# Attention whose row sums travel by DMA and whose results are divided where they lie, with new written orders for a quad of heads

## The chip, the cores and the metric

The kernel runs on one core of a Trainium2 chip. A core has five engines that run side by side, each through its own queue of instructions in program order: TensorE (PE in the profile; its weight loads are PEld), VectorE (DVE), ScalarE (ACT), GpSimd (POOL) and SyncE (SP), which here issues nearly all DMAs. Engines wait for each other by semaphores. TensorE's results go to PSUM, of which this stage uses eight banks of 128 x 512 fp32; all else lies in SBUF or in DRAM. The metric is the device time of one execution in microseconds (us), a median over runs.

## The reference

```python
mod = (_silu(c) @ w_mod).reshape(c.shape[0], 6, 1, -1)
sa, ca, ga, sb, cb, gb = (mod[:, 0], mod[:, 1], mod[:, 2], mod[:, 3], mod[:, 4], mod[:, 5])
h = _layernorm(x) * (1 + ca) + sa
x = x + ga * _A_ref(h, A_wq, A_wk, A_wv, A_wo)      # attention
h = _layernorm(x) * (1 + cb) + sb
x = x + gb * _B_ref(h, B_w1, B_b1, B_w2, B_b2)      # layernorm, 4608 wide gelu MLP

# _A_ref: 32 query heads of 18 columns, one shared key and value head
scores = einsum("bhqd,bkd->bhqk", q, k) * (Dh ** -0.5)
p = _softmax(scores, axis=-1)
o = einsum("bhqk,bkd->bhqd", p, v)
return o.transpose(0, 2, 1, 3).reshape(B, S, H * Dh) @ wo
```

All tensors are fp32. S = 2048 rows, D = 576 columns, H = 32 heads, Dh = 18.

## The kernel before, in words

The program has three stages: the first norm with the projections (to about 130 us), attention (to about 1360 us) and the MLP. The change is in attention.

**A quad.** The 2048 query rows are four blocks of 512 (tb), the 32 heads are eight quads of four heads (qd); quad n = 8 tb + qd, 32 in all. The tile qst of a quad holds its queries, split into high and low parts so that 64 rows of TensorE carry one head: rows 0 to 63 one pair of heads (g = 0), rows 64 to 127 the other (g = 1). Two of the 64 rows hold the negated maximum of each query's scores, so that the product gives the scores less the maximum.

**An order written out by hand.** The loop at the end of the listing runs for each quad through a string of tokens: QUAD for quads 0 to 8, QUADW for 9 to 30, LAST for 31. Each token is work that is issued at that place, in the same order on every engine's queue:

- S0, S1 (st_mm): one score matmul of 64 x 128 keys by 512 queries into a bank of psB (four banks), then ScalarE's exp from there into P (line 966). 64 of them a quad.
- M0, M1 (mx_mm): one score matmul of a coming quad into psM (three banks), then VectorE's maximum over it (line 986). X1 and R1 are a pair that handles two key blocks in one: ScalarE's relu of the product with a key difference (line 977), then VectorE's addition and maximum (line 984). 48 M and 8 of each of X1 and R1 a quad. The digit is g.
- V2, V3, V4 (pv_mm, line 954): two, three or four of the 64 units of P times V of a quad, each unit 128 columns of a chunk for four heads. They run eight units behind the scores. V has 32 columns of which 18 are values; the others are ones, so that row 18 of each head's 32 rows of the result is the row sum of the exponentials.
- F1, F2 (smax_fin1, smax_fin2): the maxima of the next quad. F1 reduces them on VectorE, F2 turns them on TensorE (line 358), ScalarE and VectorE write two parts, and four DMAs (line 365) put them into the next quad's qst.
- WO: one half row tile of the output projection (14 matmuls, line 753) of a finished block, and its addition to x.
- T1, RC, T2, OS: each takes post_quad (lines 763 to 803), which works off a finished quad, one step further.

After every fourth V unit, `between` issues what has no token: the load of the quad after next (load_q, six DMAs), one step of the generators in `fill` (first late_weights, then ln2_rows) and one or two steps of weight_parts, which splits the MLP's weights on GpSimd and stores them to DRAM. In the chunks named by `quiet` (the two before F2 and the one before RC) weight_parts rests.

**post_quad before.** When the last V unit of a quad is issued, ScalarE copies the result from PSUM to O (128 x 512: for each of four heads 32 rows, by 512 queries). T1: VectorE turns O in blocks of 32 x 32 (line 771), so that the row sums become column 18 of each block of T. RC: VectorE takes the reciprocal of those, GpSimd multiplies T by them (line 775). T2: VectorE turns T back into O (line 777). OS: ScalarE rounds O to fp32r (line 789), GpSimd takes the rest (line 790), and four DMAs put both into the attention tile A (lines 794 to 801).

**ln2_tile before.** When both halves of a row tile of x have their output projection, ln2_rows is added to `fill` for tiles of the first two blocks (eight tiles). ln2_tile (lines 582 to 630) takes the second norm, scales it, takes the MLP's own norm, all step by step, and then TensorE turns the 128 x 576 tile by five transposes (transpose_tile, line 156); ScalarE copies four of them from PSUM to yr, VectorE the fifth. The steps marked "T" are held back until a WO token. The tiles of the other two blocks are normed in the MLP stage by ln2_stages, where VectorE turns the tile in blocks of 32 x 32, four DMAs put it to DRAM (`turned`) so that the blocks land turned, and three DMAs fetch it into yr.

## Time and profile before

| | |
|---|---|
| median of 3 runs | 2215.54 us (2215.16 to 2216.22) |
| the profiled execution | 2216.44 us, of it span 2214.7 us |
| granted TensorE clock | 0.999 |
| instructions | 46128 |
| DMA, mean over the span | 141 GB/s |

The profile's span runs from the first to the last instruction. Busy time is the union of an engine's instructions. The page's groups name a line, the engine, the operation, what is written and read with shapes, the count, then busy time and the mean of one. A row of a timeline is a start, a duration and a group; rows of one line that follow each other are merged. An engine's idle time is put down to what ended it.

### The profile page before, as it was taken

What the parts mean: (1) busy time and instruction counts of PE and PEld (TensorE: products, weight loads), DVE (VectorE), ACT (ScalarE), POOL (GpSimd) and SP (SyncE); (2) the same over time, 40 slices, a digit from 0 to 9 for tenths busy, and PEclk for the clock granted to TensorE, in tenths of its full rate; (3) what the DMA queues carried; (4) which work ended last, traced back from release to release, by engine and by line L of the source; (5) the groups of instructions that cost most, each with busy time, mean ns of one, the idle gap of its engine ahead of it and who ended that gap; (6) DMA issues with size and microseconds to landing.
All of it is one profiled execution on the core that took longest, in us unless ns stands there. A gap on an engine that the chain in (4) does not pass through costs nothing.

```text
span 2214.7 us, 46128 instructions
## 1 busy us (share of the span) xinstructions
PE 2195.2 (99%) x16599; PEld 1446.6 (65%) x16599; DVE 1936.6 (87%) x3421; ACT 1629.8 (74%) x3122; POOL 1524.4 (69%) x1768
## 2 busy tenths in 40 slices
PE   8999999999999999999999999999999999999999
PEld 6654444444544545445454445898988899889898
DVE  7589999999999999999999992888888878787887
ACT  5579999999999999999999998544445444343443
POOL 7654456666776687677676640888899767877676
PEclk9999999999999999999999999999999999999999
DMA  6233143443333332333333321666767746676663
GB/s 228 87 133 92 34 134 117 135 130 113 126 121 120 116 130 95 114 130 112 116 117 121 127 71 59 200 195 190 201 187 201 207 131 180 184 219 189 177 184 122
DMA packets 209082, 312.71 MB, mean 141 GB/s; under 512 B 39023, under 2 KB 99839, under 8 KB 208853
## 3 DMA queue, kind: packets, MB, share of 16 engines
q1 hardware_dynamic: 208709, 309.60, 45.0%
q8 instruction: 132, 2.16, 0.4%
q14 instruction: 97, 0.79, 0.1%
q10 hardware_dynamic: 144, 0.15, 0.0%
HBM read 203.30 MB, written 96.15 MB: 135 GB/s over the span
## 4 chain that ended last, share of the span: by engine, by line
PE 96%; DVE 1%; ACT 1%; issue 1%; POOL 1%; DMA 0%; SPq 0%; ACTq 0%; DVEq 0%; POOLq 0%
PE psC L954 24%; PE psB L1178 18%; PE psA L1281 16%; PE psB L964 14%; PE psM L320 13%; PE psB L753 2%; PE psB L249 2%; PE psB L974 2%; PE psA L1315 1%; PE psA L320 1%; PE psA L753 1%; PE psB L156 0%; DVE mx L345 0%; PE psB L358 0%; PE psM L964 0%
## 5 line engine op out<-in xcount | busy, mean ns | idle before, releaser
L966 ACT ACTIVATE P<-psB 128x512 f32<-128x512 f32 x2013 | 1055.0, 620 | 42.5 <-PE psM L320 19.7
L986 DVE TENSOR_REDUCE mx<-psM 128x1 f32<-128x512 f32 x1476 | 934.3, 682 | 28.6 <-PE psM L320 13.6
L964 PE MATMUL psB<-qst,KS 64*128 64x512 f32 x2013 | 605.1, 433 | 0.1
L320 PE MATMUL psM<-KS,qst 64*128 64x512 f32 x1722 | 590.0, 434 | 0.7 <-DVE mx L338 0.2
L954 PE MATMUL psC<-P,V 128*32 128x256 f32 (+3 forms) x6608 | 568.2, 439 | 0.0
L964 PEld LDWEIGHTS psB<-qst,KS 64*128 64x128 f32 x2013 | 301.9, 184 | 218.7 <-ACT P L966 185.3
L320 PEld LDWEIGHTS psM<-KS,qst 64*128 64x128 f32 x1722 | 283.6, 184 | 185.6 <-DVE mx L986 130.9
L1178 PE MATMUL psB<-ops,w1a 128*128 128x512 f32 x1512 | 393.8, 396 | 0.2 <-DVE h L1193 0.2
L1178 PEld LDWEIGHTS psB<-ops,w1a 128*128 128x128 f32 x1512 | 270.1, 188 | 46.8 <-DVE h L1193 0.6
L954 PEld LDWEIGHTS psC<-P,V 128*32 128x32 f32 x6608 | 147.0, 108 | 187.4 <-issue 159.9
L1287 DVE TENSOR_TENSOR XT<-psA,XT 128x576 f32<-128x576 f32 x330 | 241.4, 752 | 16.2 <-PE psA L1281 10.8
L1281 PEld LDWEIGHTS psA<-w2s,big 128*128 128x128 f32 x1584 | 223.7, 188 | 12.1 <-DVE XT L1287 0.2
L1281 PE MATMUL psA<-w2s,big 128*128 128x288 f32 x1584 | 230.1, 294 | 0.0
L1255 POOL TENSOR_TENSOR big<-s,big 128x512 fp32r<-128x512 f32 x132 | 171.0, 1296 | 10.6
L984 DVE CUSTOM_DVE_ANT_0 xc<-psM,xc 128x512 f32<-128x512 f32 x246 | 166.2, 682 | 12.6 <-PE psB L964 4.6
L1191 ACT ACTIVATE psB<-gs 128x512 f32<-128x512 f32 x144 | 86.7, 602 | 120.7 <-DVE gs L1190 120.7
L1187 ACT ACTIVATE h<-psB,b1t 128x512 f32<-128x512 f32 x144 | 97.9, 680 | 105.1 <-PE psB L1178 98.6
L790 POOL TENSOR_TENSOR os<-O,os 128x512 fp32r<-128x512 f32 x31 | 39.8, 1284 | 171.4 <-ACT os L789 171.4
L977 ACT ACTIVATE xc<-psB 128x512 f32<-128x512 f32 x246 | 154.5, 628 | 2.8 <-PE psM L320 0.2
L1190 DVE SCALAR_TENSOR_TENSOR gs<-psB,h 128x512 f32<-128x512 f32 x144 | 98.9, 687 | 38.6 <-ACT psB L1188 38.5
L824 POOL TENSOR_TENSOR r<-r,r 128x256 fp32r<-128x256 f32 (+1 forms) x162 | 121.8, 752 | 13.0
L1196 ACT ACTIVATE big<-h 128x512 fp32r<-128x512 f32 x39 | 24.7, 634 | 139.5 <-DVE h L1193 139.5
(216 smaller groups left out, 3306.0 us busy)
## 6 DMA issues: line engine op xcount, KB each, us to landing
w1a<-w1scr SPq DMA_DIRECT2D x252, 256.0 KB
w2s<-w2sum SPq DMA_DIRECT2D x132, 288.0 KB
w1scr<-r SPq DMA_DIRECT2D x126, 256.0 KB
w2s<-w2scr SPq DMA_DIRECT2D x76, 288.0 KB
w2scr<-r SPq DMA_DIRECT2D x72, 288.0 KB
w2sum<-r SPq DMA_DIRECT2D x72, 288.0 KB
...
```

The costliest lines, as they stand in the source:

```text
L320: pe.matmul(o, QST[n][64 * g:64 * g + 64, p, 128 * qt:128 * (qt + 1)], KS[64 * g:64 * g + 64, 512 * kb:512 * (kb + 1)], start=True, stop=True)
L824: po.tensor_tensor(o[:, n:2 * n], src, o[:, :n].bitcast(F32), op=ALU.subtract)
L954: pe.matmul(PVt[n][32 * j:32 * (j + 1), cs], V[:, kc, :], t[:, j, cs], start=(kc == 0 and h0 == 0), stop=(kc == 15), skip_group_check=True)
L964: pe.matmul(t, KS[64 * g:64 * g + 64, 128 * kc:128 * (kc + 1)], QST[n][64 * g:64 * g + 64, i, :], start=True, stop=True)
L966: ac.activation(P[n, kc][:, 2 * i + g, :], t, AF.Exp, scale=SCALE)
L977: ac.activation(XC[-1], t, AF.Relu)
L984: ve.tensor_tensor_reduce(c, t, c, 1.0, -3.0e38, ALU.add, ALU.max, o)
L986: ve.tensor_reduce(o, t, axis=AX.X, op=ALU.max)
L1178: pe.matmul(o, x, y, start=(first and i == 0), stop=(i == len(terms) - 1), skip_group_check=True)
L1255: po.tensor_tensor(unit(u, 1), x, unit(u, 0).bitcast(F32), op=ALU.subtract)
L1281: pe.matmul(p[:, i, :288], x[:, ts_], W2S[k][:, y], start=(bool(first) and q == 0), stop=(q == 2), skip_group_check=True)
L1287: ve.tensor_tensor(o, p[:, :, :288], o, op=ALU.add)
```

## The change

- post_quad no longer turns O for quads 0 to 29. A new generator, divide, takes its place. At T1 a DMA gathers the four rows of sums (512 each) from O into R, 128 partitions of 16. At RC VectorE takes the reciprocals in place, and a DMA stores them to DRAM (rscr). At T2 a DMA reads them back, each head's row spread over its 32 partitions (T, 128 x 512). At OS GpSimd multiplies O by T where it lies.
- In these quads GpSimd also rounds O to fp32r, where ScalarE did, and a new token OD, right behind F2, issues the DMAs into A. Quads 30 and 31 go the old way.
- QUAD and QUADW are new orders of the same numbers of S, M, X, R, and of 64 V units, with OD added. LAST is unchanged.
- ln2_tile turns its tile by VectorE in place and by DMAs through DRAM, as ln2_stages does, into a new scratch turnedA. The steps "T" are gone, and so are the PE transposes and the copies from PSUM. The branch for tiles with tb of 2 or more, which this function never sees, is gone too, and with it the norm of the 64 columns that were kept twice.

```diff
+        ve.transpose(h, h)
+        yield
+        for p in range(0, 128, 32):
+            sy.dma_start(turned0.rearrange("(c f) n -> f c n", f=32)[:, :, p:p + 32],
+                         h[p:p + 32].rearrange("f (c n) -> f c n", n=32))
+        yield
+        yield
+        yr = YR[tb // 2][:, KD * (tb % 2):KD * (tb % 2 + 1), 128 * t:128 * (t + 1)]
+        sy.dma_start(yr[:, :KD - 1], turned0[:512].rearrange("(k p) n -> p k n", p=128))
+        for q in range(2):
+            sy.dma_start(yr[64 * q:64 * q + 64, KD - 1], turned0[512:])
         yield
...
+    def divide(n, O):
+
+        R = px.tile([128, 16], F32, name="R", bufs=2)
+        sy.dma_start(R, O[DH::32].rearrange("j (i c) -> j i c", c=16))
+        yield
+        ve.reciprocal(R, R)
+        sy.dma_start(rscr[n % 2].rearrange("j (i c) -> (j i) c", c=16), R)
+        yield
+        T = px.tile([128, 16, 32], F32, name="T").rearrange("p a b -> p (a b)")
+        sy.dma_start(T, rscr[n % 2][:, None, :].to_broadcast([4, 32, TB]))
+        yield
+        po.tensor_mul(O, O, T)
...
-        ac.activation(os[:, 0], O, AF.Copy)
+        if n < NQT - 2:
+            e.tensor_copy(os[:, 0], O)
+        else:
+            ac.activation(os[:, 0], O, AF.Copy)
         e.tensor_tensor(os[:, 1], O, os[:, 0].bitcast(F32), op=ALU.subtract)
+        if n < NQT - 2:
+            yield
...
-    QUAD = """S0 M0 S1 S1 M0 V3 S0 M1 S1 M0 M1 S0 V3 M0 S1 M1 S0 V2 M0 S1 S1 M0 X1 S0 V4 T1 X1 M0 M1 M0 S1 S0
-            V4 S1 RC M0 S1 S0 M0 S0 M1 V3 S0 M1 R1 S1 S0 M0 X1 V3 M0 S1 S1 R1 S0 M0 S1 V3 M0 X1 M0 S0 S1 S0
-            M1 V3 M0 S1 S1 M0 S0 R1 S0 V3 R1 S0 S1 M1 S0 M0 X1 V3 M0 S1 M0 S1 S0 S0 R1 V3 M0 X1 S0 M1 S0 M1
-            V3 S1 M0 M0 S1 T2 S0 S1 V4 M0 S1 S0 M1 S0 M1 V3 S0 R1 S1 M0 F1 S1 S0 V3 X1 M0 S1 M0 R1 S0 F2 OS
-            V4 M0 M1 S0 S1 M0 X1 V4 S1 M0 S1 S0 M1 M0 S1 V2 R1 S0 M1 S0 V2 S0 S1 M0 M1 V2 S1""".split()
-    QUADW = """M1 M1 S0 S0 X1 S1 M0 V4 S1 M0 S1 S0 M1 M0 V4 M0 S1 S0 M0 S1 T1 M0 X1 V4 S1 RC S0 S0 M1 M0 S1 V4
-            S0 R1 M1 S0 S1 M0 S1 V3 S1 M0 S0 X1 M0 M0 S1 V2 M0 S1 S0 R1 V2 M0 X1 M0 S1 S0 S1 M0 V4 S0 T2 R1
-            M0 S1 OS S0 M1 WO S0 R1 M1 S0 M1 S0 X1 V3 S0 M1 M0 S1 S1 M1 S0 V3 M0 S1 S0 R1 S0 M0 X1 V3 M0 S1
-            X1 M0 S1 M0 S1 V4 S1 M0 R1 S0 M1 S0 V4 S0 M1 M0 F1 S1 S0 S1 V4 M0 S1 M0 X1 S0 M1 F2 V4 M1 S0 S0
-            S1 M0 S1 M0 V3 R1 S0 S0 S1 R1 M0 V3 S0 S1 M0 S1 M0 S1 V3 M0 S1 M1 S0 M1 S0 V3""".split()
+    QUAD = """S1 S0 M1 S0 V4 M0 S1 M0 S1 S0 M1 V4 S1 M0 M1 S0 S1 S0 M1 V4 X1 M0 R1 S0 X1 M0 S0 T1 V3 S1 M0 S1 S0
+            M1 M0 S1 V3 M1 S0 S1 M0 X1 M0 S1 V3 M0 S1 M0 S1 S0 M1 V3 M0 S1 S0 S0 R1 M1 S0 V3 S1 M0 S0 S1 R1 S1
+            M0 V3 M0 X1 S0 S1 M1 M0 S1 V3 M1 S0 RC S0 X1 R1 M0 S1 V3 S1 M0 S0 R1 S0 M0 S1 V4 S0 M1 S0 X1 M0 X1
+            M0 T2 V4 M0 S1 M0 R1 S0 S1 S0 V4 X1 M0 S0 R1 S1 M0 OS V3 M0 S1 S0 S1 M1 S0 V4 F1 M0 S1 M0 M1 S0 S1
+            F2 OD V3 S0 R1 S0 S1 M1 S1 M0 V3 M0 S1 S1 S0 M0 M1 S0 V3 S0 M1 M0""".split()
+    QUADW = """S1 M0 S1 S0 S1 M0 V4 S1 M0 X1 M0 M1 S0 V4 S0 S1 M0 S1 S0 M1 M0 V4 S1 M0 M1 S0 S0 M0 S1 T1 V3 X1 M0
+            S1 M1 S0 R1 S0 V4 X1 M0 S1 M1 M0 S1 S0 V4 S0 M1 S0 R1 S1 M1 S0 V3 S0 R1 X1 M0 S1 S0 M1 V3 M0 S1 M0
+            X1 S1 R1 S0 V4 S0 RC S1 M0 S1 M0 M1 V3 S0 S1 S1 M0 M0 X1 V4 S0 R1 S0 R1 M0 S1 WO S0 M1 M0 M0 S1 S1
+            S0 T2 V3 M0 S1 S0 S0 M1 M0 X1 V4 S0 M1 S1 M0 S1 M0 S1 OS V3 M0 S0 M1 S0 S1 M0 F1 S1 V4 R1 S0 S1 M0
+            X1 M0 F2 OD V3 S1 M0 M1 S0 S0 S1 M0 V3 M1 S0 S0 S1 R1 M1 S0 V4 M0""".split()
```

What each order has of V tokens, groups and places:

| | QUAD before | QUAD after | QUADW before | QUADW after |
|---|---|---|---|---|
| V4, V3, V2 | 5, 12, 4 | 7, 12, 0 | 9, 8, 2 | 10, 8, 0 |
| V units done at T1, RC, T2 | 12, 16, 40 | 12, 33, 40 | 8, 12, 27 | 12, 33, 40 |
| V units done at OS, F2, OD | 50, 50, - | 48, 55, 55 | 27, 48, - | 47, 54, 54 |
| V units done at WO | - | - | 27 | 40 |

More of the change, by code (lines that the diff above doesn't have):

```diff
@@ L501, in block_kernel @@
     WO, YR, ATT, B2 = {}, {}, {}, {}
+    rscr = [dr.tile([4, TB], F32, name="rscr%d" % i) for i in range(2)]
     woscr = dr.tile([2, 128, D], F32, name="woscr")
@@ L650, in ln2_rows @@
         if tb % 2 and t == NT - 1:
+            yield
+            yield
             R = YR[tb // 2]
@@ L769, in post_quad @@
         yield
-        T = px.tile([128, 16, 32], F32, name="T")
-        ve.transpose(T.rearrange("p a b -> p (a b)"), O)
-        yield
-        R = px.tile([128, 16], F32, name="R", bufs=2)
-        ve.reciprocal(R, T[:, :, DH])
-        e.tensor_tensor(T, T, R[:, :, None].to_broadcast([128, 16, 32]), op=ALU.mult)
-        yield
-        ve.transpose(O, T.rearrange("p a b -> p (a b)"))
-        yield
+        if n < NQT - 2:
+            yield from divide(n, O)
+        else:
+            T = px.tile([128, 16, 32], F32, name="T")
+            ve.transpose(T.rearrange("p a b -> p (a b)"), O)
+            yield
+            R = px.tile([128, 16], F32, name="R", bufs=2)
+            ve.reciprocal(R, T[:, :, DH])
+            e.tensor_tensor(T, T, R[:, :, None].to_broadcast([128, 16, 32]), op=ALU.mult)
+            yield
+            ve.transpose(O, T.rearrange("p a b -> p (a b)"))
+            yield
         if tb not in ATT:
```

37 lines of the change are left out of this document (12 added, 25 removed).

## The prediction

> **What bounds the kernel now.** I read the page first, for the engine that ends last:
>
> ```profile
> PE 2195.2 (99%) x16599; PEld 1446.6 (65%) x16599; DVE 1936.6 (87%) x3421; ACT 1629.8 (74%) x3122; POOL 1524.4 (69%) x1768
> ...
> PE 96%; DVE 1%; ACT 1%; issue 1%; POOL 1%; DMA 0%; SPq 0%; ACTq 0%; DVEq 0%; POOLq 0%
> PE psC L954 24%; PE psB L1178 18%; PE psA L1281 16%; PE psB L964 14%; PE psM L320 13%; PE psB L753 2%; PE psB L249 2%; PE psB L974 2%; PE psA L1315 1%; PE psA L320 1%; PE psA L753 1%; PE psB L156 0%; DVE mx L345 0%; PE psB L358 0%; PE psM L964 0%
> ```
>
> The chain of waits is nearly all TensorE. Its attention lines (954, 964, 320, 974, 753) make some 55% of the span. A busy PE isn't a PE at its peak, so I cut the attention stage into single quads of heads, each from its first V group to the next quad's, and asked for the busy time of every engine in five of them. The columns are the stretch, its length, then PE, PEld, DVE, ACT and POOL busy, the clock, the DMA share and GB/s:
>
> ```profile
> 317.90:355.29 37.39, 37.39 (x365) 18.50 (x361) 36.54 (x71) 36.97 (x76) 25.28 (x37) 1.00 0.40 133
> 355.29:392.69 37.40, 37.40 (x365) 18.47 (x361) 36.55 (x71) 36.96 (x76) 22.44 (x36) 1.00 0.36 120
> 943.01:982.27 39.26, 39.26 (x346) 19.21 (x343) 37.86 (x75) 37.30 (x76) 31.86 (x46) 1.00 0.40 134
> 982.27:1022.19 39.92, 39.92 (x351) 19.82 (x348) 38.03 (x76) 37.86 (x77) 24.33 (x33) 1.00 0.32 105
> 1180.39:1219.65 39.26, 39.26 (x346) 19.27 (x344) 37.08 (x72) 37.28 (x76) 23.81 (x35) 1.00 0.33 111
> ```
>
> The first two follow QUAD, the others QUADW. The last and the third take the same 39.26 us although VectorE works 0.8 us less and GpSimd 8 us less in one: neither sets the length. ScalarE is within 0.4 us of it in QUAD. The fourth holds the five PE transposes of a norm tile and is 0.66 us longer.
>
> Is PE itself full? I priced its groups by where the next one starts, in the timeline of PE, and show those stretches by themselves: V4, a seven-op group (four on one half of the rows), V3, a six-op group (three and three), V2, a four-op group, and the 14 matmuls of a WO:
>
> ```profile
> 814.87:815.87 1.00, 1.00 (x11) 1.00 0.00 0
> 815.87:816.99 1.12, 1.12 (x11) 1.00 0.05 15
> 816.99:817.78 0.79, 0.79 (x11) 1.00 0.03 5
> 821.24:822.14 0.90, 0.90 (x11) 1.00 0.99 379
> 351.60:352.16 0.56, 0.56 (x9) 1.00 0.04 7
> 352.16:352.83 0.67, 0.67 (x8) 1.00 0.03 6
> 522.76:524.82 2.06, 2.06 (x16) 1.00 0.00 0
> ```
>
> S, M, X and R with digit 0 use rows 0 to 63, with digit 1 rows 64 to 127, and the halves run side by side: two, three and four in the longer half give 0.67, 0.90 and 1.12, so a group costs 0.21 + 0.23 for each in its longer half. The rest of a quad is waiting, and these rows of weight loads (stretch 470 to 1300, 21 quads) say for whom:
>
> ```profile
> L964 PEld LDWEIGHTS psB<-qst,KS 64*128 64x128 f32 x1344 | 201.4, 184 | 157.2 <-ACT P L966 139.7 <-issue 3.5 <-ACT xc L977 3.0
> L320 PEld LDWEIGHTS psM<-KS,qst 64*128 64x128 f32 x1176 | 194.9, 184 | 130.4 <-DVE mx L986 89.8 <-DVE mx L984 13.1 <-issue 12.8
> ```
>
> Loads wait for ScalarE to free psB and VectorE to free psM; most of that lies under the matmul in flight.
>
> **The orders, counted.** QUADW before has 9 V4, 8 V3 and 2 V2: 9.00 + 6.32 + 1.12 = 16.44. Its groups between them, the one with WO counted as two, are 20, with 69 in the longer halves: 4.20 + 15.87. With WO 2.06 and the transpose of the maxima 0.21 (timeline below) that is 38.78; measured 39.26, so 0.48 of waiting. After: 10 V4 and 8 V3 (16.32), 19 groups with 71 (the closing M0 joined to the next quad's first group): 3.99 + 16.33, and 2.27 again: 38.91. QUAD before: 5 V4, 12 V3, 4 V2 (16.72), 21 groups with 68 (4.41 + 15.64), 0.21: 36.98, measured 37.39, so 0.41 waiting. After: 7 V4 and 12 V3 (16.48), 19 groups with 71 (20.32), 0.21: 37.01. So the new orders give PE no less work: 0.13 more in each of 22 quads, 0.03 in 9, 2.86 + 0.27, together **+3.13 us**. They can gain only from the waiting, 22 x 0.48 + 9 x 0.41 = 14.25 us in all.
>
> **The norm tiles.** Of eight tiles these go:
>
> ```profile
> L156 PE MATMUL psB<-ident,Z x40: 270/272/274, 603.6 to 1158.3; 128*128 128x128 f32 x40
> ...
> L166 ACT ACTIVATE yr<-psB x8: 597/602/603, 604.3 to 1158.5; 128x512 f32<-128x512 f32 x8
> L168 DVE COPY yr<-psB x8: 291/292/294, 604.4 to 1158.6; 128x128 f32<-128x128 f32 x8
> ```
>
> PE gets back 39.92 - 39.26 = 0.66 each: 8 x 0.66 = **-5.28 us**, the surest term, as it comes off the bounding engine. In their place come one VectorE transpose of 128x576 and seven DMAs a tile. From 0.70 for 512 columns (below) the transpose is an estimated 0.79, so VectorE pays 0.50 net in a quad in which it drops 1.4; the cover is psM's three banks, and without it PE would lose up to those 0.50 in eight quads, 4 us. For the DMAs the stage after attention has the same step:
>
> ```profile
> L696 SPq DMA_DIRECT2D turned<-BC x32: 382/536/1148, 1473.9 to 1749.3; - x32
> ```
>
> Four puts are 2.1 us of SP's time, at the end of a quad, behind the maxima's DMAs; the rows of quads above have the DMA engines at 0.32 to 0.40. Nobody in attention reads yr, so I cost them at nothing. If they held the queue, the next quad's load would be late by those 2.1 us, and it has a quad to spare.
>
> **The division.** What goes, and its neighbours:
>
> ```profile
> L771 DVE STREAM_TRANSPOSE T<-O x21: 700/703/705, 473.1 to 1263.8; 128x512 f32<-128x512 f32 x21
> L774 DVE RECIPROCAL R<-T x21: 231/234/238, 474.3 to 1265.0; 128x16 f32<-128x16 f32 x21
> L775 POOL TENSOR_TENSOR T<-T,R x21: 1042/1048/1060, 477.5 to 1265.8; 128x512 f32<-128x512 f32 x21
> L777 DVE STREAM_TRANSPOSE O<-T x21: 654/700/704, 482.8 to 1273.5; 128x512 f32<-128x512 f32 x21
> ```
>
> ```profile
> L794 SPq DMA_DIRECT2D big<-os x76: 764/800/886, 486.2 to 1279.5; - x76
> L789 ACT ACTIVATE os<-O x21: 632/661/672, 484.1 to 1274.8; 128x512 fp32r<-128x512 f32 x21
> L790 POOL TENSOR_TENSOR os<-O,os x21: 1276/1285/1305, 484.8 to 1275.6; 128x512 fp32r<-128x512 f32 x21
> ```
>
> VectorE drops 0.70 twice, ScalarE 0.66. GpSimd multiplies two full tiles (as L790, 1.29) instead of T by R (1.05), and copies os:
>
> ```profile
> L823 POOL CAST r<-w2b 128x288 fp32r<-128x288 f32 x85 | 36.0, 424 | 20.7 <-DMA w2scr<-r 8.7 <-DMA w2sum<-r 6.7 <-DMA w1scr<-r 2.8
> ```
>
> That is 0.42 x 512/288 = 0.75, so +1.0 us a quad on 31.9 of 39.3: hidden, until GpSimd passes PE. Three DMAs are new. The trace has no gather of 64-byte pieces and no such broadcast; the nearest are the four small qst<-ms below (0.70 to issue, about 1.4 to land) and, for the 256 KB broadcast, a load of 72 KB on the chain:
>
> ```profile
> 40.90 3.53 DMA qst<-qscr
> ```
>
> So 2.1 to 3.5 us each, perhaps 5 for the broadcast; I take 3.5, the larger transfer. The tokens leave 21 of 64 V units (12.9 us) for the gather and 7 (4.3 us) for the store, and 4.3 for the broadcast. The reciprocal waits for the gather with the maxima behind it, but with 9 us to spare; the multiply waits with only GpSimd's weight parts behind it, which has 7 us idle a quad. Cost: nothing, and none below, since PE touches no part of it.
>
> What it buys is waiting. ScalarE's 0.66 and VectorE's 1.4 are each more than the 0.41 or 0.48 to be had, but in QUAD ScalarE is still at 36.3 of 37.0, so not all goes. I take three quarters: 14.25 x 0.75 = **-10.69 us**, an estimate between none and all.
>
> **The maxima's way to the next quad** is what the new orders tighten. The rows of PE, of SP, and of a tenth of a microsecond in which the last of four DMAs moves:
>
> ```profile
> 814.66 0.28 PE L358 MATMUL psB<-ident,mxf 128*16 128x128 f32 x1
> 814.87 1.06 PE L954 MATMUL psC<-P,V 128*32 128x512 f32 x8
> ...
> 823.21 0.47 PE L964 MATMUL psB<-qst,KS 64*128 64x512 f32 x1
> ```
>
> ```profile
> 816.06 2.79 SPq L365 DMA_DIRECT2D qst<-ms  x4
> ```
>
> ```profile
> 819.50:819.60 0.10, 0.10 (x6) 0.05 (x2) 0.10 (x3) 0.10 (x1) 0.00 (x0) 1.00 0.21 36
> ```
>
> From the transpose (F2) to landing: 819.60 - 814.66 = 4.94 us; the next quad's first score comes 3.6 us later still. After the change QUADW has behind F2 only 0.21, V3, seven, V3, seven, V4: 0.21 + 0.79 + 1.12 + 0.79 + 1.12 + 1.00 = 5.03, and QUAD 4.82 and one 0.23 step. So 0.1 us is left of 3.6. I cost it at nothing; what it costs beyond that is a rival.
>
> The last of the four is issued at 816.06 + 2.79 - 0.70 = 818.15, so its data move 1.45 us after the issue, and by these rows the margin holds. The Trainium skill, "DMA: Bandwidth & Descriptors", section "Anatomy of one DMA — SWDGE (gpsimd) path", gives one DMA some 2.0 us of fixed time, most of it the wait for the receipt of the write, and so speaks against this edit. By that figure, an estimate from that page, the last row would be there at 820.15, 5.49 behind F2 and 0.46 past the margin, and the sum would be 2199.1 (rival 1) + 31 x 0.46 = 2213.4; the burst speaks for less, but shows data and no receipt.
>
> **Sum.** The profiled execution took 2216.44 us (span 2214.7), 0.9 above the median of the runs: 2216.44 + 3.13 - 5.28 - 10.69 = 2203.60, or 2202.7 as a median.
>
> **Rivals.**
> 1. All the waiting goes: 2215.5 + 3.1 - 5.3 - 14.25 = 2199.1. My prices are read to 0.01 us, and half of that in 37 groups of 31 quads is 5.7: 2193. For it: both engines are relieved by more than the wait. Against: ScalarE's 98% in QUAD.
> 2. The waiting stays, being a matter of three or four banks: 2215.5 + 3.1 - 5.3 = 2213.3. For it: VectorE's 0.8 less between two quads above moved nothing.
> 3. The burst shows the data move, not PE being told. If that came a quarter of the way from the burst's 1.45 to the 3.53 that the chain shows for a landing, 0.52 us later, it would be 0.43 past the margin. PE standing there lets the others catch up, so it adds to 2199.1: 31 x 0.43 = 13.3, 2212.4. For it: the chain's row; against it: that row moves more bytes. The Trainium skill's rule of the receipt, on the page named above, is of this kind.
> 4. Slower: SP isn't free when the maxima are ready, behind the broadcast, a store or a put that waits. Each 0.1 us past the margin costs 3.1; one foreign issue of 0.80 and 0.2 of queue give 31 us: 2230. It makes the kernel slower by 0.2% from 0.67 past the margin. Against it: no weight part is stepped in the two chunks before F2, and the broadcast goes out 14 V units (8.6 us) ahead.
> 5. Gather or broadcast late enough to hold VectorE or GpSimd: it would need 9 us more; left out of the sum.
>
> **How the numbers follow.** Forecast 0.57 (2199 to 2209), rival 1 0.21, rival 2 0.10, rival 3 0.05, rival 4 0.07. About 0.2%, 4.4 us, is what a measurement here can tell. Forecast and rival 1 are faster than 2211.1: 0.78; rivals 2 and 3 within: 0.15; rival 4 slower: 0.07. The range runs from rival 1's 2193 to rival 2's 2213.3, a little rounded up; only rival 4 is outside.
>
> **What would show it.** Right: quads of one length, with no 0.66 us extra in every second one; QUADW near 39.0 and QUAD near 37.1; ScalarE down 0.6 and VectorE 1.4 a quad; no weight load of a quad's first score waiting for qst<-ms. Wrong: that load waiting 0.3 us or more (rivals 3, 4), or PE's loads waiting for L966 and L986 as long as now (rival 2), or the reciprocal waiting for its gather.

## The result, and the profile after

| | us, median of the runs | runs | profiled execution | its span |
|---|---|---|---|---|
| before | 2215.95 (2215.16 to 2216.22) | 6 | 2216.44 | 2214.7 |
| after | 2223.31 (2222.62 to 2226.99) | 6 | 2226.99 | 2225.2 |

The ratio is 1.0035 [1.0025, 1.0046]: slower by 7.4 us, where 13.3 us less was forecast. The profiled execution of after is 3.7 us above its median, so single stalls in it count for more than in the usual run.

The page of after, engines and chain:

```profile
PE 2201.3 (99%) x16711; PEld 1450.5 (65%) x16711; DVE 1906.4 (86%) x3361; ACT 1620.8 (73%) x3084; POOL 1549.0 (70%) x1790
...
PE 86%; DVE 5%; POOL 1%; ACT 1%; DMA 1%; issue 0%; SPq 0%; DVEq 0%; ACTq 0%; POOLq 0%
...
L984 PE MATMUL psB<-qst,KS 64*128 64x512 f32 x2013 | 607.0, 433 | 3.5 <-DMA qst<-ms 3.5
...
L773 POOL TENSOR_TENSOR O<-O,T 128x512 f32<-128x512 f32 x30 | 38.6, 1288 | 182.1 <-DMA T<-rscr 96.9
```

VectorE and ScalarE did become lighter (DVE 1936.6 to 1906.4 us, ACT 1629.8 to 1620.8). But TensorE's part of the chain, 96% before, is 86% now: VectorE has 5% of it, and the first score of a quad waits for the maxima's DMA (3.5 us in all). GpSimd's product waits for the broadcast row sums (96.9 us in all), most of it off the chain.

The same cut into quads, with the columns of the prediction: quad 5, which follows QUAD; quads 11 and 12; quads 20 and 21, an even and an odd one, over which a norm tile's steps are spread; and quad 27, which has no tile:

```profile
321.37:358.99 37.62, 37.62 (x339) 18.13 (x338) 35.22 (x69) 36.79 (x75) 26.15 (x38) 1.00 0.42 139
551.21:591.76 40.55, 40.14 (x361) 19.83 (x360) 36.52 (x72) 37.25 (x75) 32.09 (x41) 1.00 0.38 125
591.76:632.93 41.17, 40.63 (x362) 20.12 (x360) 37.84 (x74) 37.46 (x76) 30.99 (x47) 1.00 0.47 144
912.23:951.93 39.70, 39.60 (x361) 19.88 (x360) 36.67 (x73) 37.15 (x76) 22.94 (x36) 1.00 0.45 136
951.93:991.87 39.94, 39.83 (x361) 19.57 (x361) 37.25 (x74) 37.21 (x76) 33.99 (x42) 1.00 0.38 127
1190.82:1230.13 39.31, 39.31 (x362) 19.68 (x360) 36.08 (x71) 37.02 (x75) 23.21 (x35) 1.00 0.38 123
```

Three things are to be seen. Quad 27 has nothing of a tile in it and takes 39.31 us where the quad of before took 39.26, although VectorE works 1.0 us less: the waiting did not go. Quads 20 and 21 are .4 and .6 longer than it, and so are the others with a tile's steps, where before only every second one was. And quads 11 and 12 lose over a microsecond each. The prediction's view of TensorE's weight loads (stretch 470 to 1300) has become lighter all the same:

```profile
L984 PEld LDWEIGHTS psB<-qst,KS 64*128 64x128 f32 x1335 | 200.8, 184 | 152.6 <-ACT P L986 100.8 <-issue 18.1 <-ACT xc L997 17.6
L321 PEld LDWEIGHTS psM<-KS,qst 64*128 64x128 f32 x1168 | 187.7, 184 | 99.5 <-DVE mx L1006 60.5 <-DVE mx L1004 17.0 <-issue 4.0
```

The idle time that ends on the exponentials fell from 139.7 to 100.8 us, that on the reductions from 89.8 to 60.5, and no quad without a tile is shorter for it. Most of this idle time lies under a matmul in flight, so its sum doesn't tell what a quad would gain. The traces show four causes of the new loss.

**The tile's step on VectorE.** Quad 21 again, VectorE and then TensorE's weight loads, in order of time (the bracket is the idle time before, and what ended it):

```profile
986.52 0.27 DVE L362 SCALAR_TENSOR_TENSOR ms<-psB,ms 16x128 fp32r<-16x128 f32 x1
986.72 0.76 DVE L616 STREAM_TRANSPOSE Z<-Z 128x576 f32<-128x576 f32 x1
987.41 2.43 DVE L1006 TENSOR_REDUCE mx<-psM 128x1 f32<-128x512 f32 x4
```

```profile
988.11 0.18 PEld L321 LDWEIGHTS psM<-KS,qst 64*128 64x128 f32 x1 [0.68 <-DVE mx L1006]
...
988.71 0.18 PEld L321 LDWEIGHTS psM<-KS,qst 64*128 64x128 f32 x1 [0.30 <-DVE mx L1006]
989.30 0.18 PEld L321 LDWEIGHTS psM<-KS,qst 64*128 64x128 f32 x1 [0.42 <-DVE mx L1006]
```

```profile
988.11:989.74 1.63, 1.52 (x11) 0.67 (x8) 1.63 (x3) 1.50 (x4) 1.55 (x3) 1.00 0.03 5
```

Chunk 13's step comes just behind F2, when VectorE has done the reduction and the split of the maxima and has the reductions of a whole group still to do. TensorE's loads for psM wait for these reductions, and the group of seven behind the step, whose price is 1.12, takes 1.63. In the even quads it is the two pieces of statistics (0.66 us) that stand there, and the same group takes 1.58. That is .5 us in 14 quads, 7 us.

**The maxima's landing.** Between quads 27 and 28: the transposition of the maxima (F2), the last of the four DMAs on SyncE's queue, and the weight load of the next quad's first score:

```profile
1223.69 0.28 PE L359 MATMUL psB<-ident,mxf 128*16 128x128 f32 x1
```

```profile
1227.33 0.63 SPq L366 DMA_DIRECT2D qst<-ms  x1
```

```profile
1229.20 0.18 PEld L984 LDWEIGHTS psB<-qst,KS 64*128 64x128 f32 x1
```

The data move until about 1228.70, 1.37 behind the issue, as this stretch of a tenth of a microsecond shows (the DMA share is the last column but one; in the next tenth it is 0.01):

```profile
1228.60:1228.70 0.10, 0.10 (x4) 0.00 (x0) 0.10 (x3) 0.10 (x1) 0.00 (x0) 1.00 0.22 41
```

The load comes 1.87 us behind the issue, .50 behind the data, and 5.51 behind F2, where the orders leave 5.03 by the prices. The ends of quads 9 to 11 and 26 to 30 all have 1.87 or 1.88. Not all of these .48 are the landing's. In the version below with both edits, the last issue comes 1.5 us sooner and nothing waits for it. There F2 of quad 27 stands at 1208.68, and the same load at:

```profile
1213.92 0.18 PEld L982 LDWEIGHTS psB<-qst,KS 64*128 64x128 f32 x1
```

That is 5.24 behind F2. So the landing holds the load back by .27, and quads 27 to 29 are longer by .1 and less for it (39.31, 39.30 and 39.23; 39.21, 39.25 and 39.23 with the maxima in two DMAs). Quad 30, behind whose F2 no maxima are left, so that TensorE comes to the next score sooner, is .87 longer (38.24 and 37.37). For quad 2 the four rows came later still; this piece of the chain (start, length) runs from the last issue to the landing, and TensorE stood idle for 1.58 of it, in quad 1:

```profile
202.33 3.45 DMA qst<-ms
```

Two weight loads of 1440 KB each, issued before it on the same queue, were just ending. Whether they held it is not shown: in the second run below the same place has 1.87, with the same loads and the same four DMAs. Quad 2 lost another 1.4 us (39.31; 37.87 before), and not by a wait. The column before the DMA share is the granted clock:

```profile
207.50:210.91 3.41, 3.41 (x18) 1.03 (x14) 1.89 (x3) 2.07 (x5) 3.33 (x2) 0.50 0.41 135
```

Such a stretch of 3.41 us at half clock follows a stall of TensorE in three of the versions below too, 1.2 to 1.8 us after it works again: behind 2.74 us of idle TensorE (old tile, quad 25), 2.06 (chunk 13's step left out, quad 16) and 1.18 (old division, quad 25). At half clock it costs up to 1.7 us, so a long single stall costs more than its own length. The rule isn't found: in the second of these versions a stall of 1.65 us in quad 25 was not followed by one.

**The gather.** Quad 11, VectorE and SyncE's queue:

```profile
570.50 0.25 DVE L767 RECIPROCAL R<-R 128x16 f32<-128x16 f32 x1 [1.25 <-DMA R<-O]
```

```profile
566.13 0.34 SPq L848 DMA_DIRECT2D w1scr<-r  x1
...
567.87 0.61 SPq L765 DMA_DIRECT2D R<-O  x1
```

The gather was issued only at 567.87: SyncE had stood until 566.13 at a store of the weight parts (L848) that waited for GpSimd, and the reciprocal, with the maxima queued behind it, then waited 1.25 us for the row sums. TensorE lost 1.18. **GpSimd late for the tile**, quad 12:

```profile
592.09 0.78 DVE L616 STREAM_TRANSPOSE Z<-Z 128x576 f32<-128x576 f32 x1 [1.16 <-POOL Z L593]
```

```profile
586.43 1.28 POOL L773 TENSOR_TENSOR O<-O,T 128x512 f32<-128x512 f32 x1 [4.27 <-DMA T<-rscr]
```

GpSimd waited 4.27 us for the broadcast, at the end of quad 11, with the tile's norm queued behind it, and VectorE then waited 1.16 us for the norm in quad 12: 1.48 on TensorE.

### The profile page after: what moved, and what is told of

It is laid out like the page before. It is cut to its first block, busy times and chain, and to the rows that moved or that the text cites. A ratio compares the mean times of both kernels' runs of the same rounds, so it can differ in the third digit from the quotient of the medians.

```text
span 2225.2 us, 46588 instructions
## 1 busy us (share of the span) xinstructions
PE 2201.3 (99%) x16711; PEld 1450.5 (65%) x16711; DVE 1906.4 (86%) x3361; ACT 1620.8 (73%) x3084; POOL 1549.0 (70%) x1790
## 4 chain that ended last, share of the span: by engine, by line
PE 86%; DVE 5%; POOL 1%; ACT 1%; DMA 1%; issue 0%; SPq 0%; DVEq 0%; ACTq 0%; POOLq 0%
PE psC L974 21%; PE psB L1198 18%; PE psA L1301 16%; PE psB L984 13%; PE psM L321 11%; DVE mx L1006 3%; PE psB L752 2%; PE psB L994 2%; PE psA L1335 1%; PE psA L752 1%; ACT P L986 1%; DMA qst<-ms 0%; PE psB L250 0%; DVE xc L1004 0%; DMA T<-rscr 0%
## 5 line engine op out<-in xcount | busy, mean ns | idle before, releaser
L321 PE MATMUL psM<-KS,qst 64*128 64x512 f32 x1722 | 597.5, 436 | 2.5 <-DVE mx L1006 0.6
L974 PE MATMUL psC<-P,V 128*32 128x512 f32 (+3 forms) x6760 | 561.2, 433 | 0.0
L974 PEld LDWEIGHTS psC<-P,V 128*32 128x32 f32 x6760 | 154.9, 108 | 195.0 <-issue 164.8
L1301 PEld LDWEIGHTS psA<-w2s,big 128*128 128x128 f32 x1584 | 223.7, 188 | 12.2 <-DVE XT L1307 0.2
L773 POOL TENSOR_TENSOR O<-O,T 128x512 f32<-128x512 f32 x30 | 38.6, 1288 | 182.1 <-DMA T<-rscr 96.9
L997 ACT ACTIVATE xc<-psB 128x512 f32<-128x512 f32 x246 | 149.2, 611 | 1.6
```

Source lines behind the costliest of these rows:

```text
L321: pe.matmul(o, QST[n][64 * g:64 * g + 64, p, 128 * qt:128 * (qt + 1)], KS[64 * g:64 * g + 64, 512 * kb:512 * (kb + 1)], start=True, stop=True)
L974: pe.matmul(PVt[n][32 * j:32 * (j + 1), cs], V[:, kc, :], t[:, j, cs], start=(kc == 0 and h0 == 0), stop=(kc == 15), skip_group_check=True)
L997: ac.activation(XC[-1], t, AF.Relu)
L1301: pe.matmul(p[:, i, :288], x[:, ts_], W2S[k][:, y], start=(bool(first) and q == 0), stop=(q == 2), skip_group_check=True)
```

## The experiments

The theory after these traces: the waiting that the prediction wanted to remove does not depend on VectorE's and ScalarE's sum over a quad but on how a group's evictions stand against its few banks, so that a lighter quad buys nothing; and the new steps cost what their places make of them. The rival: the lighter engines do buy the forecast's 10.7 us, and the four new waits eat it.

### Taking the new waits away

Old norm tile in the changed kernel (`ln2_tile` as before: the five transposes by TensorE, evicted by ScalarE and VectorE).

> The changed kernel with the norm tile turned by TensorE again; division and orders stay new. Theory A (the tile's VectorE steps fall behind F2, where psM has no slack, and cost 0.5 us in each of 14 quads; behind them the maxima's rows land too late for the next quad, 0.25 us a quad where no stall hides it): eight times 0.66 us of PE transposes come back (+5.3), 14 x 0.5 = 7.0 and the 2.7 us around the first tile go, the landing shows in those 14 quads (+3.5): about 2222 us, and the quads that hold no transpose at 39.3 us. Theory B (the tile is innocent, the new orders and the division's DMAs cost it): 2223.3 + 5.3 = 2228.6.

Measured 2231.18 us (2230.11 to 2232.78), ratio to before 1.0072 [1.0058, 1.0086]. Neither theory: the version with the new tile is 7.9 us faster in the new orders. TensorE's transposes cost .58 in each of eight quads, and the gather was late in six quads of the trace, worst in quad 25, where the reciprocal waited 3.7 us for it behind a store that had held SyncE for 6.6 us; with the half clock behind it that quad takes 44.55. The gather's place has no margin against SyncE's order, and what else GpSimd does decides in which quads that shows.

The step of chunk 13 left out, in the quads with a WO group:

```diff
-        if kc % 2 and (held[0] != "T" or not pieces):
+        if kc % 2 and (n <= NQ or kc != 13) and (held[0] != "T" or not pieces):
```

> The changed kernel, but no step of the norm tile in chunk 13, the one behind F2; its steps come one odd chunk later. Theory A: the 0.5 us stall in the group before the last goes in 14 quads, but the wait for the maxima's rows, about 0.25 us, appears in its place: 2223.3 - 3.5 = 2219.8. If the landing isn't a bound: 2223.3 - 7.0 = 2216.3. Theory B: 2223.3.

Measured 2220.99 us (2219.08 to 2224.99), 1.0024 [1.0014, 1.0034]. The 14 stalls are gone from the trace (most of the tile's quads are at 39.3 to 39.5), but the tile's puts now meet the gather: in quad 16 the reciprocal waited 3.4 us, by the profile for the put `turnedA<-Z`, and that quad lost over 4 us, the half clock behind the stall included; quads 15, 18 and 25 lost .5, .7 and 1.9. 2.3 us of the 7 were kept. The time is near theory A's, but not for its reason: the wait for the maxima's rows did not grow to .25 in the tile's quads (39.31 here, 39.23 in the version below with both edits).

The maxima in two DMAs instead of four:

```diff
-        for g in range(2):
-            for s in range(2):
-                r = 64 * g + R3 + s
-                sy.dma_start(QST[n][r:r + 1].rearrange("o p (t c) -> o (p t) c", c=128).bitcast(F32),
-                             ms[8 * g:8 * (g + 1), s].bitcast(F32))
+        for s in range(2):
+            sy.dma_start(QST[n][R3 + s::64].rearrange("g p (t c) -> g (p t) c", c=128).bitcast(F32),
+                         ms[:, s].bitcast(F32))
```

> The changed kernel with two DMAs for the maxima's rows in place of four, so that the last is issued some 1.4 us sooner. Theory A: the quads of QUAD lose their wait of 0.3 to 0.6 us and the second one up to 1.4 of its 2, the quads of QUADW without a tile 0.25, those with a tile nothing, since VectorE's stall stands there: 2223.3 - 5 = 2218. Theory B, or if the landing were early enough: 2223.3.

Measured 2218.38 us (2217.62 to 2219.05), 1.0011 [1.0002, 1.0020]. Theory A's figure: two issues fewer, 1.3 us of SyncE, and the margin holds. That is 4.9 us less, but not all of it is the landing's. The two traces differ by .87 in quad 30, by .44 and .49 in quads 4 and 7, by .18 and less in the others whose rows landed late: 2.7 us in all. Quads 11 and 12 are shorter by 1.16 and .48: no reciprocal waits for the gather any more, and the transposition waits .66 for GpSimd, not 1.16. Quads 1 and 2 are at 38.11 and 37.73 after 39.90 and 39.31, but this doesn't count for the two DMAs: in the run before this one, with four, they take 38.22 and 37.81. Their 3.4 us, the late rows and the half clock, are most of what the profiled execution of after took above its median.

Both edits:

> Both edits. Theory A (two waits one behind the other, each hiding the other): both go, 2223.3 - 7.0 - 5 = 2211, more than the sum of the two alone. If they were independent: the sum of the single gains, 2214.8 by the numbers above. Theory B: 2223.3.

Measured 2211.09 us (2210.95 to 2211.56), 0.9979 [0.9970, 0.9987]: faster than both kernels, and 12.2 us below the changed one. Together the two gains are more than their sum apart, and the time is theory A's figure, but not for its reason: against the run with the step alone left out, most of the tile's quads gain less than .1. What goes beside quad 30's .95 are the single stalls, with the half clock behind one of them, in quads 15, 16, 18 and 25 (from 40.03, 43.62, 40.02 and 41.41 to 39.51, 39.23, 39.23 and 39.52), 7.6 us. That the DMAs saved are on the queue which the puts and the gather share would explain it, and was not tried by itself. The quads of this version, 5, 27, and 20 and 21 of the tiles:

```profile
317.00:354.49 37.49, 37.49 (x339) 18.27 (x339) 35.53 (x69) 36.79 (x76) 26.56 (x39) 1.00 0.43 140
1175.81:1215.04 39.23, 39.23 (x361) 19.65 (x360) 36.02 (x70) 37.18 (x76) 28.66 (x38) 1.00 0.37 123
900.29:939.56 39.27, 39.27 (x362) 19.62 (x361) 36.81 (x72) 37.23 (x76) 27.49 (x39) 1.00 0.45 137
939.56:979.06 39.50, 39.50 (x361) 19.75 (x361) 37.12 (x75) 37.17 (x76) 31.42 (x43) 1.00 0.38 128
```

With every new wait but one (.27 in the odd tile quads) gone, QUADW is at 39.23 and not at 39.0, and QUAD at 37.49. So the rival falls: the new waits had not eaten a gain of 10.7 us.

The tile's steps kept out of chunk 11 as well, with two pauses fewer in the tile:

```diff
+        if kc % 2 and (n <= NQ or kc not in (11, 13)) and (held[0] != "T" or not pieces):
```

> The 2211.09 us version with the tile's steps kept out of chunk 11 as well as 13 in the quads with a WO group, and the tile's pauses cut by two, so that a tile still fits two quads: its VectorE steps then fall in chunks 15, 1, 7, 9 and 3. Theory A: the .29 us by which the odd quads of the tiles are longer (39.51 against 39.22, the group with F2 at 1.43) comes from a tile step just ahead of F1 and goes; the steps find slack elsewhere: 7 or 8 x .29 = 2.2 us less, 2208.9. Theory B: VectorE has no slack anywhere in these orders and each .66 to .8 us step costs about .3 wherever it stands: 2211 again. Rival C: the put and the get of the tile now meet the sums' DMAs on SyncE, and single quads lose 1 us and more: 2213 to 2216.

Measured 2216.81 us (2215.69 to 2217.64), 1.0004 [0.9995, 1.0012]: worse by 5.7. Quads 20 and 21:

```profile
903.83:943.55 39.72, 39.69 (x360) 19.59 (x360) 36.82 (x71) 37.21 (x76) 31.43 (x45) 1.00 0.44 133
943.55:982.78 39.23, 39.23 (x361) 19.57 (x360) 37.27 (x76) 37.20 (x76) 30.63 (x41) 1.00 0.42 137
```

The odd quads lost their .27, as theory A had it, but the transposition, which came to lie at the end of chunk 5, makes a group take 1.56 in the even ones that took 1.18 in the version before this one, and quad 11 lost 2.1. The same .77 us of VectorE costs TensorE .50 at chunk 13 (1.63 against 1.13 for the group), .45 at chunk 5 (39.72 against 39.27 for the quad), and in the version before this one, where it lies at the end of chunk 3 of the even quads, nothing that the rows show (39.27 there, 39.23 without a tile).

### Each part alone

The new norm tile in the kernel before:

> The kernel before with one part of the change alone: the norm tile is turned by VectorE and goes through DRAM, instead of TensorE's five transposes; orders and division stay the old ones. Theory A, the prediction's count: the 8 quads that hold TensorE's transposes lose .66 us each and nothing takes their place, 2215.9 - 5.3 = 2210.6. Theory B, from the changed kernel's trace: the .8 us step of VectorE is queued ahead of the maxima's reductions and holds TensorE by about half a us in each of the 8 tiles (and the two pieces of statistics already lay there before), so 2210.6 + 4 = 2214.6, no gain that can be told from none. Rival C: in the old orders the step stands elsewhere and meets a slack VectorE, and only the .66 goes; that is A's number, with the group around the transposition at its usual length in the trace.

Measured 2213.68 us (2213.27 to 2215.09), 0.9991 [0.9982, 0.9999]. Between A and B. Quads 20 and 21:

```profile
901.93:941.25 39.32, 39.32 (x346) 19.08 (x344) 37.61 (x75) 37.30 (x76) 28.45 (x38) 1.00 0.33 107
941.25:980.73 39.48, 39.48 (x345) 19.35 (x343) 38.22 (x76) 37.36 (x76) 29.24 (x41) 1.00 0.45 138
```

The even quads fell from 39.91 to 39.32 (-.6, as counted), the odd ones rose from 39.26 to 39.48, with a group at chunk 5 at 1.33. Single quads (12 and 22) lost .3 and .4.

The division alone, in the old orders (every score, maximum and value product where it was; T1, RC, T2, OS and OD at the chunks that the new orders give them):

> The kernel before with one part of the change alone: the row sums by DMAs and the division where the result lies, in the old orders (every score, maximum and value group as before; only the division's own places are moved to the chunks at which the new orders have them: gather 3, reciprocal 8, broadcast 10, product 12, stores 14) and with the old norm tile by TensorE. Both reliefs together took .58 us off a quad of the kernel before. Theory A: in the old orders, which were searched with the turns in them, VectorE's 1.4 us a quad and ScalarE's .6 are worth something: a third to a half of the .58 goes, 29 x .2 to .29 = 6 to 8 us, 2208 to 2210. Theory B: as in the new orders, where VectorE's whole relief bought .16 a QUADW quad and .05 a QUAD quad: at most .1 a quad, 2213 to 2216. Rival C: the gather or the broadcast comes late in single quads, behind stores that wait on GpSimd, and takes back what there is: 2216 or more, with single quads 1 us longer.

Measured 2216.64 us (2215.65 to 2218.58), 1.0003 [0.9994, 1.0012]: nothing. The figure is rival C's, the quads are theory B's: in the profiled execution, which is 1.9 above the median, quads 0 and 1 are longer by 1.2 and 1.0 (quad 0 has 3.41 us at half clock, from 133.76), and quads 3 to 29 take 1055.02 us in both traces. Quads 5 and 27, and then the weight loads of the prediction's view (stretch 470 to 1300):

```profile
320.82:358.29 37.47, 37.47 (x364) 18.36 (x363) 35.49 (x69) 36.48 (x75) 26.49 (x39) 1.00 0.40 135
1183.13:1222.36 39.23, 39.23 (x346) 19.13 (x344) 35.91 (x70) 36.78 (x75) 24.71 (x38) 1.00 0.39 127
```

```profile
L978 PEld LDWEIGHTS psB<-qst,KS 64*128 64x128 f32 x1346 | 201.7, 184 | 157.0 <-ACT P L980 139.3 <-issue 3.5 <-ACT xc L991 2.7
L320 PEld LDWEIGHTS psM<-KS,qst 64*128 64x128 f32 x1178 | 195.8, 184 | 134.2 <-DVE mx L1000 95.4 <-DVE mx L998 13.1 <-issue 12.8
```

In quad 27 VectorE went from 37.08 to 35.91 us and ScalarE from 37.28 to 36.78, TensorE's order is the same, and the quad went from 39.26 to 39.23; the QUAD quad from 37.39 to 37.47. The loads wait for ScalarE as long as before (139.3 us after 139.7), and for VectorE's reductions no less (95.4 after 89.8). Nor did the added work on GpSimd slow the others down: an exponential takes 617 ns in both traces, a plain reduction 682 and 683. The turns that went had stood in places where, by these rows, TensorE did not wait for them.

The reverse, the division put back to VectorE's turns in the 2211.09 us version (GpSimd keeps the rounding to fp32r):

```diff
-        if n < NQT - 2:
-            yield from divide(n, O)
+        if n < 0:
+            yield from divide(n, O)
```

> The version with the fill step of chunk 13 left out and the maxima in two DMAs (2211.09 us), with the division put back to VectorE's turns in every quad, the new orders and the new norm tile kept: VectorE's load goes up by about 1.1 us a quad again, the DMAs of the row sums go. Theory A, the prediction's waiting: what VectorE and ScalarE carry decides .3 to .5 us of a quad, so that the old division costs 28 quads x .3 to .4, about 9 us: 2220. Theory B: VectorE's load does not bind in these orders outside of the groups around F1 and F2, and giving it back changes the quads by at most .1: 2211 to 2214. Rival C: the sums' DMAs hold the division late in single quads (as at the quad in which the tile's turn waited 1.0 us), and the old division is then 1 us faster: 2210.

Measured 2229.46 us (2228.31 to 2229.83), 1.0059 [1.0046, 1.0071]: 18.4 us worse, worse than any of the three expected. Quads 5 and 27, and one group of seven by itself, in quad 28, the second behind the first turn:

```profile
319.67:357.70 38.03, 37.94 (x340) 18.22 (x339) 36.46 (x71) 36.90 (x76) 26.16 (x39) 1.00 0.39 130
1192.67:1232.28 39.61, 39.61 (x361) 19.71 (x360) 36.89 (x72) 37.11 (x76) 27.46 (x36) 1.00 0.35 115
1241.37:1242.85 1.48, 1.48 (x11) 0.77 (x8) 1.48 (x5) 1.09 (x3) 1.34 (x3) 1.00 0.85 246
```

The QUADW quad is .38 longer, and that one group has nearly all of it: 1.48 instead of 1.12, with VectorE busy throughout. The QUAD quad is .54 longer; quad 25 lost 3.9 us (43.39 after 39.52), where the second turn waited 2.0 us for GpSimd's product and half clock followed. The new orders leave no slack at T1 for a turn of .70 us, the old ones had it there. So the new orders depend on the new division, and the division is worth nothing in the old orders and 18 us in the new ones, 3.9 of them in one quad.

### Is there waiting at all?

The kernel before, with ScalarE's exponential and VectorE's plain reductions over 448 of 512 columns (VectorE fills the rest of the tiles once with ones, ahead of attention):

```diff
-        ac.activation(P[n, kc][:, 2 * i + g, :], t, AF.Exp, scale=SCALE)
+        ac.activation(P[n, kc][:, 2 * i + g, :448], t[:, :448], AF.Exp, scale=SCALE / 4)
-            ve.tensor_reduce(o, t, axis=AX.X, op=ALU.max)
+            ve.tensor_reduce(o, t[:, :448], axis=AX.X, op=ALU.max)
```

> The kernel before with the same relief of ScalarE and VectorE (exponential over 448 of 512 columns, maxima's reductions over 448; the output is not the reference's), orders, division and norm tile as they were. Theory A: the 14.25 us of waiting that the prediction counted (.48 in 22 QUADW quads, .41 in 9 QUAD quads) goes: QUADW 38.8, QUAD 37.0, time 2201.7. Theory B: TensorE's own time, 2215 with QUADW 39.2 and QUAD 37.4. If a part goes, its size is what waiting there was in the kernel before, and so the most that any relief of these two engines could have bought.

Measured 2205.29 us (2204.65 to 2206.21), 0.9951 [0.9938, 0.9965]; the filling holds the first value product back by 8.8 us (with 10.24 us at half clock from 134.74 on), and from there to the end of quad 29 it takes 1147.0 us instead of 1164.0. Quads 5 and 27, and one group of six and one of seven in quad 28:

```profile
325.07:361.89 36.82, 36.82 (x364) 16.97 (x362) 34.10 (x71) 34.68 (x76) 25.74 (x38) 1.00 0.41 135
1174.11:1212.80 38.69, 38.69 (x345) 18.37 (x344) 34.49 (x73) 34.85 (x76) 23.63 (x35) 1.00 0.33 112
...
1217.84:1218.78 0.94, 0.94 (x11) 0.65 (x8) 0.94 (x4) 0.88 (x2) 0.83 (x2) 1.00 0.48 161
1233.50:1234.61 1.11, 1.11 (x12) 0.71 (x8) 0.92 (x3) 1.01 (x4) 0.95 (x3) 1.00 0.44 102
```

The same two groups in the kernel before, and with the division alone changed:

```profile
1224.89:1226.00 1.11, 1.11 (x10) 0.69 (x7) 1.11 (x4) 1.11 (x4) 0.80 (x1) 1.00 0.60 169
1240.87:1242.04 1.17, 1.17 (x12) 0.84 (x8) 1.14 (x3) 1.17 (x4) 1.01 (x3) 1.00 0.44 105
```

```profile
1227.36:1228.47 1.11, 1.11 (x12) 0.71 (x8) 0.61 (x2) 1.11 (x4) 1.03 (x3) 1.00 0.60 198
1243.32:1244.49 1.17, 1.17 (x11) 0.83 (x8) 1.14 (x3) 1.17 (x4) 0.00 (x0) 1.00 0.00 0
```

So the waiting was there, .57 us a quad, even more than the .48 and .41 of the prediction, and its count of TensorE's own work stands within .2 (38.78 counted, 38.69 here; 36.98 and 36.82). It lies in small pieces, .06 in this group of seven and up to .17 in one place, and goes when each eviction (an exponential or a reduction, which empties a bank) becomes shorter: the groups of seven that take 1.16 to 1.22 in quads 5 and 27 of the kernel before take 1.11 to 1.13 here, which is the prediction's price. It does not go when the division's work goes: in the third pair the group of six has VectorE busy for .61 instead of 1.11 us and takes 1.11 all the same, with ScalarE busy throughout.

The same relief in the 2211.09 us version:

> The same version (2211.09 us), with ScalarE and VectorE relieved without a touch on TensorE's work: the exponential is taken over 448 of a score tile's 512 columns (the rest of the tile is filled once with ones, ahead of attention, and the scale is a quarter so that nothing overflows), and the maxima's plain reductions run over 448 of 512. The output is not the reference's. Both engines do about a tenth less in a quad. Theory A, the prediction's: what a QUADW quad is longer than its count by the prices of the groups (39.23 - 38.91 = .32 us) and a QUAD quad (37.47 - 37.01 = .46) is waiting for these two engines, and it goes: 22 x .32 + 9 x .46 = 11 us, 2200, with QUADW quads at 38.9 and QUAD at 37.0. Theory B: it is TensorE's own time in these sequences of score and value groups, which no relief takes away: QUADW 39.2, QUAD 37.4 and 2209 to 2211 (the .33 of the odd tile quads at most goes, 7 x .33 = 2.3 us).

Measured 2204.22 us (2203.64 to 2204.90), 0.9945 [0.9930, 0.9960], with a start 9.3 us later; 1147.0 us for the 30 quads after 1161.1. By the quads below this is theory A, and somewhat more. ScalarE alone, and VectorE alone:

> The 2211.09 us version with ScalarE alone relieved: the exponential over 448 of 512 columns, with the rest of the tiles filled once with ones (by VectorE, ahead of attention, which puts the first value product some 9 us later as in the run with both reliefs, so the quads are to be read, not the time). The output is not the reference's. With both reliefs the QUADW quads went from 39.23 to 38.79 and the QUAD quads from 37.47 to 36.78. Theory A, waits end on ScalarE, which is busy for 37.2 of 39.2 us: this relief alone brings QUADW to 38.9 or less and QUAD to 36.9 or less. Theory B, on VectorE's catching up after F1 and F2: QUADW 39.1 and QUAD 37.3 at least. If both are halves of it, 39.0 and 37.1.

> The 2211.09 us version with VectorE alone relieved: the maxima's plain reductions over 448 of 512 columns (the scale is a quarter so that nothing overflows; the output is not the reference's). VectorE gets some 3 us a quad lighter, more than twice what the division's move took off it. Theory A (ScalarE ends the waits): only the groups behind F1 and F2 gain, .1 to .2 a quad: QUADW 39.1, QUAD 37.3, and with the tiles' .29 in eight quads about 2206. Theory B (VectorE): QUADW 38.85, QUAD 36.85, and 2198. This run says what any further relief of VectorE could have bought in these orders.

2213.64 us (2212.51 to 2214.55) with the late start, 0.9989 [0.9979, 0.9998], and 2205.72 us (2204.80 to 2206.48), 0.9953 [0.9937, 0.9968]. Quads 5 and 27 of the three, first both, then ScalarE, then VectorE:

```profile
324.29:361.04 36.75, 36.75 (x339) 17.08 (x339) 32.72 (x70) 34.28 (x75) 26.62 (x39) 1.00 0.44 142
1172.42:1211.18 38.76, 38.76 (x362) 19.23 (x361) 33.05 (x71) 34.49 (x75) 29.65 (x39) 1.00 0.38 125
```

```profile
324.50:361.48 36.98, 36.98 (x339) 17.14 (x338) 35.46 (x69) 34.30 (x75) 26.63 (x39) 1.00 0.43 142
1179.28:1218.33 39.05, 39.05 (x361) 19.17 (x360) 36.04 (x70) 34.53 (x75) 30.75 (x41) 1.00 0.38 126
```

```profile
317.14:354.55 37.41, 37.41 (x338) 17.64 (x337) 32.78 (x69) 36.77 (x76) 26.46 (x39) 1.00 0.43 141
1171.27:1210.33 39.06, 39.06 (x361) 20.11 (x360) 33.04 (x71) 37.12 (x76) 29.71 (x40) 1.00 0.37 124
```

Three microseconds off VectorE, more than twice what the division took, buy .17 in QUADW and .08 in QUAD; 2.5 to 2.7 off ScalarE buy .18 and .51. For ScalarE neither theory holds: QUADW is at the figure of two halves (39.05), QUAD nearer to theory A's (36.98). In QUADW both together buy .47, more than .18 and .17. In QUAD most waits end on ScalarE, as the prediction's 98% had it, and the division could not touch its 64 exponentials. VectorE's relief did end the .27 of the odd tile quads (39.07 in this run's trace), and so its time is the 2206 that theory A gave.

### The old orders with the rest

The changed kernel with the maxima in two DMAs and the old orders:

> The changed kernel with the maxima in two DMAs and with the old orders (the division's places moved as in the run beside it): new division and new norm tile, old order of scores, maxima and value products, so F2 stands 12 chunks into a quad and not 13.5. Theory A: the tile alone gave 2.2 us in the old orders, and the division's gain adds to it: 2206 to 2208. Theory B: the tile's 2.2 us alone, 2211 to 2214. If the new orders themselves were worth anything with the new division, this is slower than the 2218.38 us that the changed kernel takes with the maxima in two DMAs.

Measured 2213.15 us (2212.57 to 2214.99), 0.9986 [0.9978, 0.9995], theory B: the tile's gain and nothing more. With the new orders the same kernel takes 2218.38. And with chunk 13's step left out too:

> The same with the fill step of chunk 13 left out in the quads with a WO group, as in the 2211.09 us version. In the old orders F2 stands at chunk 12, and VectorE's .8 us step of chunk 13 comes when it has just caught up, so theory A has nothing left to shift: within 1.5 us of the run beside it. Theory B: VectorE is behind there too, and the shift saves the same 4 to 7 us as in the new orders.

Measured 2219.53 us (2219.14 to 2221.16), 1.0017 [1.0008, 1.0026]: 6.4 us worse, outside of both theories. Two groups of the tile's quads, at chunks 1 and 9, behind the transposition and the statistics that were moved on, now take 1.46 and 1.52 instead of .90 and 1.17. The same edit that gains 7.3 us in the new orders loses 6.4 in the old ones.

## Why the prediction was wrong

**The step that failed is the last of "The division": three quarters of 14.25 us of waiting, -10.69 us.** The waiting was real (.57 us a quad), but the division alone buys none of it: 39.26 to 39.23, 37.39 to 37.47, 2216.64 us. The prediction set VectorE's 1.4 us and ScalarE's .66 a quad against .48 of waiting, as if a wait were paid from a quad's sum. The runs show it in single groups, and gone when each eviction is shorter, not when a quad has fewer other steps; that each group waits for the few banks it needs is the account that fits them. Rival 2, "a matter of three or four banks", was right on this point, and the prediction's own first rows had said it: VectorE's 0.8 less between two quads moved nothing. In the new orders, with every new wait but one gone, the quads are at 39.23 and 37.49, against the 39.0 and 37.1 that this step needed.

**"Cover is psM's three banks, without it up to .50 in eight quads, 4 us"** was costed at nothing. The count was wrong: .51 and .46 in 14 quads, 7 us, since the tile's statistics were moved to the same place in the other quads. That the price came out is in part luck: it was a difference of busy times (.79 - .29), and what TensorE pays is set by the place, nothing to .5 for the same step. Leaving chunk 13 out gave 7.3 us (2218.38 to 2211.09).

**The margin of the landing**, 0.1 us, costed at nothing: rival 3's wait is there. It put the word to TensorE .52 behind the data, and the trace has .50; as the .52 is a quarter of the way between two other figures, that is luck. The data themselves move 1.37 us after the issue and not 1.45: the last of the four DMAs of before was issued at 818.23, its issue taking .63 and not .70. The loss of .43 a quad did not come: the orders' own time behind F2 is 5.24 and not 5.03, which leaves .27 for the load, and in quads 27 to 29 .1 us and less for the quad, since a wait on TensorE lets the other engines catch up, as the prediction said. Two DMAs gained 4.9 us and not 13.3: some 2.7 us are the landing's, with .87 in quad 30, and most of the rest lies in quads 11 and 12, which had waited for the gather and the broadcast.

The Trainium skill's 2.0 us of fixed time ("DMA: Bandwidth & Descriptors", "Anatomy of one DMA — SWDGE (gpsimd) path") is given there for GpSimd's path; carried over to SyncE's, it had given 5.49, an estimate from that page. The trace has 5.51. Part of this is luck: the trace has 1.87 from the issue to the load, and a last issue .15 later behind F2 than the prediction took it.

**Rivals 4 and 5** happened in single quads: the boundary of quads 1 and 2 (late rows, 3.45 us of the chain, in the profiled execution), quad 11 (the gather), quad 12 (the broadcast, then the tile). "With 9 us to spare" counted the DMA's own time and left out that SyncE issues in order, behind stores that wait for GpSimd.

**The norm tiles** (-5.28): nearly all of the .66 went in each of eight quads (39.91 to 39.32), and .2 came back in the odd ones; alone it gave 2.2 us in the old orders (2213.68; the kernel before took 2215.85 beside it). **The orders' count** (+3.13): by the relieved quads 22 x (38.76 - 38.69) + 9 x (36.75 - 36.82) = +0.9; the sign was right, and the size is small either way.

Together: 2202.7 + 10.7 (waiting) + 7.0 (chunk 13) + 4.9 (what two DMAs gained) = 2225.3, 2.0 above what was measured. The smaller count of the orders is of that size; but the .2 of the odd tile quads is left out of this sum, and the two edits interact, so it is a check of the sizes and no proof. Of the list of what would show it, "ScalarE down 0.6 and VectorE 1.4 a quad" came halfway (.26 and 1.0 in quad 27), QUADW at 39.0 and QUAD at 37.1 did not, and two signs of wrong, the first score's load and the reciprocal waiting, are in the trace. The third, PE's loads waiting for ScalarE and VectorE as long as now, is not (100.8 us after 139.7, 60.5 after 89.8), although rival 2, for which it was to speak, was right on the waiting: it was no sign of what a quad takes.

What stays open: whether a shorter eviction helps because a bank comes free sooner or because the engines read the banks less; the relief changes both. Open too are why two issues fewer ended the late gathers, and when a stall is followed by half clock. Which places of an order have slack for a step of VectorE was found here by moving steps, not worked out from the order.
